# A fused attention and expert-routing kernel: V loads on ScalarE's queue, a fixed place for loads, stores and constants, and a new order of the attention stage

## The chip, the core and the metric

The kernel runs on one core of a Trainium2 chip. The engines that matter here are TensorE (PE in the profile, with its weight loads as PEld), VectorE (DVE), ScalarE (ACT), GpSimd (POOL) and SyncE (SP), which only issues DMAs in this kernel. The metric is the device time of one execution in microseconds; lower is better.

## The reference, cut to what matters

```python
def _attn_ref(q, k, v, w_phi):            # q, k, v: 8 x 8 x 576 x 64, f32
    def phi(x):
        proj = einsum('bhsd,df->bhsf', x, w_phi)               # 128 features
        proj = proj - max(abs(proj), axis=-1, keepdims=True)
        return concatenate([exp(proj), exp(-proj)], axis=-1)
    q_p, k_p = phi(q), phi(k)
    kv = einsum('bhsf,bhsd->bhfd', k_p, v)
    z = sum(k_p, axis=2)
    num = einsum('bhsf,bhfd->bhsd', q_p, kv)
    den = einsum('bhsf,bhf->bhs', q_p, z)[..., None] + 1e-06
    return num / den
```

The result, 4608 tokens of 512 numbers, goes through a mixture of eight experts: each token is assigned greedily by its largest gate logit, each expert takes at most 576 tokens, and each expert computes `relu(x @ w1) @ w2` for its own. The change touches only the attention stage; the expert stage after it has the same code before and after.

## The kernel before, in words

**Units.** The attention stage runs over 16 units, each a pair of batches and a pair of heads. The steps of a unit `u` are named in the function `unit`, and these names stand in the order table and in the prediction:

- `ldk`, `ldq`, `ldv`: the loads of k, q and v. K and Q come as eight DMAs each (L122), V as two (L128). `st` is the store of the attention output to the DRAM tensor `xs` (L313), one DMA. The input tiles `ki`, `qi`, `vi` and the output tile `xp` have two buffers each.
- `kt0`, `kt1`, `qt0`, `qt1`: 32x32 block transposes of k and q on VectorE (L175).
- `kg0` to `kg2`, `qg0` to `qg2`: the projections with w_phi on TensorE (L186), each over three of the nine token groups. Each is followed by `kgm`/`qgm`, the largest absolute value (L190, VectorE), and `kgs`/`qgs`, the subtraction (L193, VectorE). For `kg0` and `kg1`, from the second unit on, the subtraction is split: `kgc` copies out of PSUM on ScalarE (L199) and `kgs` subtracts on GpSimd (L202).
- `ke0` to `ke2`: the exponentials of k on ScalarE (L214). `ad1` to `ad8`: GpSimd's running sum of them (L222, L223). `kv0` to `kv2`: k_p times v on TensorE (L232).
- `kvt` (ScalarE, L236), `bd` (TensorE, L248), `kz` (ScalarE, L251): copy kv out, append the gate columns, copy back. `z` (TensorE, L263) folds the sum of `ad8`, and `zk` (VectorE, L265) puts it beside `kz`.
- `T0` to `T2`: transposes of the q projections on TensorE (L276), then `ex0` to `ex2`, their exponentials (ScalarE, L280).
- `num0`, `num1`: the numerator and denominator on TensorE (L293), then `x0`, `x1`, the division into `xp` on VectorE (L297, L298, L308); `lg` adds the gate logits on GpSimd (L318, L320).
- `init0` to `init18`: the routing stage's constants, a generator of small VectorE instructions and GpSimd iotas (`moe_consts`, L385 to L449), one piece at a time. `pr0` to `pr5`, `cnt0` to `cnt2` and `n0`: a part of the routing that is done early, for the first 27 of 36 token tiles.

**Order.** `Plan.order` decides the order in which instructions are emitted. Each step has an engine, a duration, dependencies and a due time; with the table `ATT['o']` present the plan is strict, so each engine takes its steps in the order of their due times, `16*u` plus the table's entry (`place`, L150). The engines run their own streams in that order and wait only on semaphores, so whatever stands behind a waiting step on its engine waits too. The table has one column for unit 0, one for unit 1, one for unit 15 and `s` for the others. PSUM for the stage is four pairs of banks, the tiles `g0` to `g3`; every TensorE step but `kv1` and `kv2` takes a pair and holds it until the step that reads it out is done.

The steady order before, from the due times in column `s` (a number after a name is the part, `+` marks a step of the next unit):

```
TensorE: kv0  kg1+ kg0+ kv1  kg2+ kv2  z  qg2+ bd  qg0+ qg1+ num0 num1 T2+ T1+ T0+
ScalarE: ke0 ke1 ke2 ex2 ex0 ex1 kgc1+ kgc0+ kvt kz
VectorE: zk  qgm0+ qgm1+ qgs0+ qgs2+ qgs1+ x0 x1 kt0++ kt1++ qt0++ qt1++ kgm1++ kgm0++ kgm2++ kgs2++ qgm2++
SyncE:   ldk 10, ldv 9, ldq 10, st 7, ldk 11, ldv 10, ldq 11, st 8, ...   (with ldq 15 between ldq 8 and st 5)
```

## Time and profile before

| | |
|---|---|
| median of 3 timed runs | 798.92 us (796.99 to 800.79) |
| the profiled execution, device time | 796.87 us |
| its span, first to last instruction | 795.1 us |
| mean granted TensorE clock | 0.978 |
| attention stage, to the end of the last `num1` | 296.1 us of the span |

The profile's page gives busy time and share by engine, the span in 40 slices of 19.9 us, and DMA queues. The timeline gives instructions in order, neighbours of one kind merged, with the idle time before them in brackets and what ended it. The chain of work follows the end of the program back, step by step, to what released it; there a stage is booked from the end of the one before it. "issue" stands where an engine waited for nothing that the profile shows.

### The profile page before, as it was taken

To read this page: it belongs to the slowest core of one execution; us is meant where nothing else is said; L and a number is where in the kernel's file an instruction comes from. 1 tells how busy PE (TensorE), PEld (TensorE's weight loads), DVE (VectorE), ACT (ScalarE), POOL (GpSimd) and SP (SyncE) were. 2 spreads that over 40 slices of the span, in tenths; PEclk is the share of its full clock that TensorE was granted. 3 is DMA by queue.
4 is the path that set the end of the run, shared out by engine and by line. 5 is a ranking of instruction groups with operands and counts; after the bars stand their busy time and mean duration, and the time that the engine had idled before them with its cause. 6 is when DMAs were issued, how large, how long until landed. Compare 5 with 4: busy or idle time off the path is not lost.

```text
span 795.1 us, 25101 instructions
## 1 busy us (share of the span) xinstructions
PE 750.4 (94%) x10718; PEld 651.2 (82%) x10718; DVE 546.5 (69%) x1343; ACT 349.4 (44%) x609; POOL 308.0 (39%) x327
## 2 busy tenths in 40 slices
PE   5999999899999986899999999999999999999995
PEld 3888888688888875598898898898898898897983
DVE  7998788598889857876686686685685685550400
ACT  2766667476766750343333333333333333441410
POOL 5887777688887850303203103104104104302011
PEclk9999999899999995899999999999999999999998
DMA  9767877867785311535505414423433334701200
GB/s 126 118 116 160 161 136 138 158 137 140 134 164 111 93 33 31 167 107 163 169 1 175 159 39 154 139 73 122 139 102 105 127 106 147 246 1 58 109 28 33
DMA packets 206655, 91.89 MB, mean 116 GB/s; under 512 B 154784, under 2 KB 189632, under 8 KB 206544
## 3 DMA queue, kind: packets, MB, share of 16 engines
q1 hardware_dynamic: 195712, 70.74, 37.5%
q0 software_dynamic: 6096, 18.97, 7.1%
q8 instruction: 84, 1.38, 0.7%
q10 hardware_dynamic: 4736, 0.59, 0.7%
q14 instruction: 27, 0.22, 0.1%
HBM read 71.39 MB, written 18.87 MB: 114 GB/s over the span
## 4 chain that ended last, share of the span: by engine, by line
PE 69%; issue 13%; DVE 5%; POOL 4%; SPq 3%; DMA 3%; ACT 1%; POOLq 0%; DVEq 0%; ACTq 0%
PE h L849 20%; PE y L878 17%; PE g L293 7%; PE g L232 7%; PE g L186 6%; SPq L122 3%; PE g L276 3%; PE y L893 2%; PE h L824 2%; POOL out_dram L907 1%; PE rps L602 1%; DMA qi<-in_q_dram 1%; POOL ks L223 1%; PE rps L598 1%; PE g L248 1%
## 5 line engine op out<-in xcount | busy, mean ns | idle before, releaser
L223 POOL TENSOR_TENSOR ks<-ks,kP 128x512 f32<-128x512 f32 x112 | 143.3, 1279 | 9.1 <-ACT kP L214 0.6
L849 PE MATMUL h<-xh,w1h 128*128 128x272 f32 (+3 forms) x512 | 144.5, 303 | 0.2 <-DVE xl L827 0.2
L849 PE MATMUL h<-xh,w1l 128*128 128x272 f32 (+3 forms) x512 | 142.9, 299 | 0.0
L907 POOL DMA_INDIRECT out_dram<-ysb,idx x40 | 40.4, 1010 | 206.2 <-ACT ysb L901 166.6
L860 ACT ACTIVATE fh<-h 128x272 fp32r<-128x272 f32 (+2 forms) x128 | 49.2, 384 | 134.7 <-PE h L849 123.6
L819 POOL DMA_INDIRECT xg<-xs,idx x40 | 39.5, 986 | 177.2 <-issue 141.3
L878 PE MATMUL y<-w2h,fl 128*128 128x512 f32 x256 | 102.1, 399 | 0.0
L878 PE MATMUL y<-w2l,fh 128*128 128x512 f32 x256 | 101.9, 398 | 0.0
L878 PE MATMUL y<-w2h,fh 128*128 128x512 f32 x256 | 101.3, 396 | 0.0
L849 PEld LDWEIGHTS h<-xh,w1h 128*128 128x128 f32 x512 | 96.4, 189 | 2.1 <-issue 1.2
L849 PEld LDWEIGHTS h<-xh,w1l 128*128 128x128 f32 x512 | 96.6, 189 | 0.0
L849 PE MATMUL h<-xl,w1h 128*128 128x272 f32 (+3 forms) x512 | 91.7, 298 | 0.0
L864 DVE SCALAR_TENSOR_TENSOR fl<-h,fh 128x272 fp32r<-128x272 f32 (+2 forms) x128 | 52.8, 420 | 55.8 <-ACT fh L860 42.4
L280 ACT ACTIVATE qP<-g 128x768 f32<-128x768 f32 x96 | 70.0, 828 | 41.9 <-PE g L276 41.9
L293 PE MATMUL g<-kz,qP 128*64 128x73 f32 x2304 | 78.5, 227 | 0.3 <-issue 0.3
L293 PEld LDWEIGHTS g<-kz,qP 128*64 128x64 f32 x2304 | 75.3, 136 | 3.7 <-issue 3.0
L214 ACT ACTIVATE kP<-kgt 128x768 f32<-128x768 f32 x96 | 72.7, 836 | 11.1 <-DVE kgt L193 10.5
L849 PEld LDWEIGHTS h<-xl,w1h 128*128 128x128 f32 x512 | 75.6, 188 | 0.0
L232 PE MATMUL g<-kP,vi 64*64 64x256 f32 x1152 | 73.2, 384 | 1.1 <-DVE xp L308 0.7
L901 ACT COPY ysb<-y 128x512 f32<-128x512 f32 (+1 forms) x40 | 21.8, 544 | 97.3 <-PE y L878 64.1
L232 PEld LDWEIGHTS g<-kP,vi 64*64 64x64 f32 x1152 | 44.1, 135 | 15.8 <-issue 3.9
L190 DVE TENSOR_REDUCE kgm<-g 128x6 f32<-128x768 f32 x48 | 44.5, 951 | 17.6 <-PE g L186 17.5
(195 smaller groups left out, 1340.1 us busy)
## 6 DMA issues: line engine op xcount, KB each, us to landing
raww<-in_moe_w_dram SPq DMA_DIRECT2D x64, 512.0 KB, 5.8
vi<-in_v_dram SPq DMA_DIRECT2D x32, 288.0 KB, 4.8
xs<-xp SPq DMA_DIRECT2D x16, 576.0 KB, 4.3
ki<-in_k_dram SPq DMA_DIRECT2D x124, 72.0 KB, 3.6
qi<-in_q_dram SPq DMA_DIRECT2D x124, 72.0 KB, 3.7
xg<-xs,idx POOLq DMA_INDIRECT x40, 3.5
out_dram<-ysb,idx POOLq DMA_INDIRECT x40, 2.9
ki<-in_k_dram ACTq DMA_DIRECT2D x4, 72.0 KB, 4.1
```

Of the source, the lines that this page charges most:

```text
L186: PE.matmul(p[64*bi:64*bi+64,a,128*(s-s0):128*(s-s0)+128],t[r,bi,s,:],C['w'][r,:],start=True,stop=True)
L190: V.tensor_reduce(m,vw(),axis=AX.X,op=OP.max,apply_absolute_value=True)
L214: for i in range(2): A.activation(o[:,:,:,128*i:128*i+128],t,AF.Exp,scale=1.0-2*i)
L223: else: G.tensor_add(ks,ks,kP[:,s])
L232: PE.matmul(p[64*a:64*a+64,i,0:256],v_[r,a,s,:],kP[r,s,a,:],start=s==0,stop=s==8,skip_group_check=True)
L280: for fh in range(2): A.activation(t[:,fh].rearrange('p a s t -> p a (s t)'),p,AF.Exp,scale=1.0-2*fh)
L293: PE.matmul(p[64*ab:64*ab+64,a,73*(j-j0):73*(j-j0)+73],T['qP',u,j//3][:,fh,a,j%3,64*ab:64*ab+64],T['kz',u][:,ab,fh,a,:],start=fh==0,stop=f ...
L849: PE.matmul(p,ws[:,k,o:o+128],xx[:,k,o1:o2],start=n==0,stop=n==11)
L860: A.activation(hh[:,f,o1:o1+m1],p[:,0:m1],AF.Relu)
L864: V.scalar_tensor_tensor(hl[:,f,o1:o1+m1],p[:,0:m1],0.0,hh[:,f,o1:o1+m1],op0=OP.max,op1=OP.subtract)
L878: PE.matmul(p,hx[:,f,o:o+128],ws[:,f%2,:],start=n==0,stop=n==23)
L907: st=G.indirect_dma_start(out=ov,out_offset=bass.IndirectOffsetOnAxis(ap=iv,axis=0),in_=yv,in_offset=None)
```

## The change

Five things change in the code. The V loads of units 1 to 15 are issued on ScalarE's queue instead of SyncE's. Every SyncE step takes its place from column `s`, in all units, so the first and the last unit's loads and stores stand where a middle unit's do. The 19 pieces of routing constants get due times of -100 to -82 and so stand first on VectorE. The planner's cost of a DMA issue, of unit 0's projections, of an init piece and of an instruction fetch (`fetch`, 3700 to 4200) change; these are numbers in the plan and no instructions. The table `o` is replaced.

```diff
@@ loadv
-            nc.sync.dma_start(t[64*i:64*i+64].rearrange('p h s d -> p h (s d)'),o)
+            (nc.scalar if u else nc.sync).dma_start(t[64*i:64*i+64].rearrange('p h s d -> p h (s d)'),o)
@@ place
-        return u*16.+t[{0:'0',1:'1',NU-1:'9'}.get(u,'s')][(name if isinstance(name,str) else ''.join(map(str,name)))+'.'+eng]
+        return u*16.+t['s' if eng=='SP' else {0:'0',1:'1',NU-1:'9'}.get(u,'s')][(name if isinstance(name,str) else ''.join(map(str,name)))+'.'+eng]
@@ unit
-            add('ldk','SP',5200.,-d['ldk'],lambda x: loadx('k',k,u),slot=slots(('ki',2)),lat=4500.)
-            add('ldq','SP',5200.,-d['ldq'],lambda x: loadx('q',q,u),slot=slots(('qi',2)),lat=4500.)
-            add('ldv','SP',1300.,-d['ldv'],lambda x: loadv(u),slot=slots(('vi',2)),lat=4500.)
+            add('ldk','SP',6000.,-d['ldk'],lambda x: loadx('k',k,u),slot=slots(('ki',2)),lat=5000.)
+            add('ldq','SP',6000.,-d['ldq'],lambda x: loadx('q',q,u),slot=slots(('qi',2)),lat=5000.)
+            add('ldv','ACT',1300.,-d['ldv'],lambda x: loadv(u),slot=slots(('vi',2)),lat=5000.)
...
-            add((nm,g),'PE',n*218.,due,pe,[(src[0]+'t',0),(src[0]+'t',1)],'Q',slots(('g',NG,nm,g)),((src,u),),ins=16*n+.5)
+            add((nm,g),'PE',n*(218. if not first else 480. if nm=='kg' else 340.),due,pe,[(src[0]+'t',0),(src[0]+'t',1)],'Q',slots(('g',NG,nm,g)),((src,u),),ins=16*n+.5)
...
-        P.add(('init',i),'DVE',330.,place(('init',i),'DVE',0,d['init']),some,[('init',i-1)] if i else [],lat=95.,after=3900.)
+        P.add(('init',i),'DVE',270.,-100.+i,some,[('init',i-1)] if i else [],lat=95.,after=3900.)
@@ ATT
...
```

The new column `s` puts the steps in this order (the same signs):

```
TensorE: kg0 kg1 kv0- kg2 qg2 kv1- qg0 kv2- qg1 bd- z- T2 T0 num0- num1- T1      (- is the unit before)
ScalarE: kgc0 kgc1 ldv ke0 kvt- kz- ke1 ex2 ex0 ke2 ex1
VectorE: kgm0 qt1 kgm1 kgm2 kgs2 qgm2 qgm0 qgs2 qgs0 kt0+ zk- qgm1 kt1+ qgs1 qt0+ x0- x1-
GpSimd:  kgs0 ad8- kgs1 ad1 ad2 ad3 ad4 lg-- ad5 ad6 ad7     (-- is two units before)
SyncE:   ldk 10, st 6, ldq 10, ldk 11, st 7, ldq 11, ...      (ldq 15 stands after st 11)
```

At the start VectorE's order is `init0` to `init12`, `kt0`, `init13`, `kt1`, `init14` to `init17`, `qt0`, `init18`, `kgm0`, `qt1` of unit 0; before, it was `init0` to `init9`, `kt0`, `kt1`, `init10`, `init11`, `kgm0`, `kgm1`, with `init12` to `init18` spread over units 1 to 4. At the end TensorE's order is `num0 num1` of unit 14, `qg1 kv0 kv1 kv2 qg2 T1 bd cnt0 cnt1 cnt2 z T2 num0 num1` of unit 15; before, `num0 num1` of unit 14, `T2 kv0 qg1 qg0 kv1 kv2 T1 T0 bd cnt0 cnt1 z cnt2 num0 num1`.

## Rows read from the trace of the kernel before

**Rows 1.** The page: busy time and share by engine with counts, the instruction queue with packets, MB and share, and one group of section 5 (busy us, mean ns of one, idle time before it).

```profile
PE 750.4 (94%) x10718; PEld 651.2 (82%) x10718; DVE 546.5 (69%) x1343; ACT 349.4 (44%) x609; POOL 308.0 (39%) x327
...
q8 instruction: 84, 1.38, 0.7%
...
L214 ACT ACTIVATE kP<-kgt 128x768 f32<-128x768 f32 x96 | 72.7, 836 | 11.1 <-DVE kgt L193 10.5
```

**Rows 2.** Busy time of each engine in a stretch of the attention stage: window, length, PE, PEld, DVE, ACT, POOL with counts, granted clock, DMA share, GB/s.

```profile
68.00:261.00 193.00, 184.11 (x4880) 162.09 (x4872) 160.42 (x248) 126.65 (x177) 150.59 (x132) 0.98 0.75 144
```

**Rows 3.** The chain of work that ended last: start, length, what. The L293 rows are `num0` and `num1` of units 2, 5, 7, 13 and 15, the L276 rows one and two of the steps `T`; the DMA row is a store of the attention output on its way.

```profile
68.41 4.72 PE g L293 x144
...
119.73 4.72 PE g L293 x144
...
141.93 3.83 DMA xs<-xp
...
159.85 4.72 PE g L293 x144
...
261.05 4.83 PE g L293 x144
...
280.69 0.80 PE g L276 x6
...
286.85 1.46 PE g L276 x12
...
291.35 4.74 PE g L293 x144
```

**Rows 4.** Timeline of TensorE's matmuls over one unit in the middle: start, length, line, operation, count. A step is read from its start to the start of the next, since the ends overlap.

```profile
172.51 0.59 PE L263 MATMUL g<-one,ks 64*64 64x2 f32 x32
172.95 0.86 PE L186 MATMUL g<-w,qT 64*64 64x128 f32 x24
173.64 0.68 PE L248 MATMUL g<-bd,kvT 64*64 64x72 f32 x32
174.14 1.83 PE L186 MATMUL g<-w,qT 64*64 64x128 f32 x48
175.90 4.79 PE L293 MATMUL g<-kz,qP 128*64 128x73 f32 x144
180.62 2.19 PE L276 MATMUL g<-ident,qgt 128*128 128x128 f32 x18
182.74 1.53 PE L232 MATMUL g<-kP,vi 64*64 64x256 f32 x24
...
187.34 1.48 PE L232 MATMUL g<-kP,vi 64*64 64x256 f32 x24
188.63 0.59 PE L263 MATMUL g<-one,ks 64*64 64x2 f32 x32
```

**Rows 5.** Timeline of ScalarE in the unit after, with the idle time before an instruction and its releaser in brackets.

```profile
186.10 1.66 ACT L199 COPY kgt<-g 128x768 f32<-128x768 f32 x2 [0.24 <-DVE kgm L190]
188.88 0.58 ACT L236 COPY kvT<-g 128x512 f32<-128x512 f32 x1 [1.12 <-PE g L232]
190.50 0.65 ACT L251 COPY kz<-g 128x576 f32<-128x576 f32 x1 [1.04 <-PE g L248]
```

**Rows 6.** Timeline of SyncE's queue from the loads of unit 8 on: start, time from the first issue of the row to the end of the last, line, count.

```profile
126.81 1.29 SPq L128 DMA_DIRECT2D vi<-in_v_dram  x2
128.21 13.68 SPq L122 DMA_DIRECT2D qi<-in_q_dram  x16
141.93 0.63 SPq L313 DMA_DIRECT2D xs<-xp  x1
```

**Rows 7.** Timeline of TensorE's matmuls in the same stretch.

```profile
146.94 1.51 PE L276 MATMUL g<-ident,qgt 128*128 128x128 f32 x6 [3.75 <-DVE rd L297]
```

**Rows 8.** Timeline of TensorE's weight loads where "issue" ended an idle time.

```profile
85.00 0.95 PEld L186 LDWEIGHTS g<-w,qT 64*64 64x64 f32 x33 [1.80 <-issue]
```

**Rows 9.** Timeline of VectorE: pieces of the routing constants.

```profile
47.40 2.07 DVE L437 TENSOR_SCALAR dup<-dup,msk 128x128 bf16<-128x128 bf16 x2
...
64.18 1.44 DVE L442 TENSOR_SCALAR idp<-idi 128x36 int32<-128x36 int32 x1 [0.86 <-POOL idi L441]
65.54 0.17 DVE L443 TENSOR_SCALAR idp<-idi 128x36 int32<-128x36 int32 x1
```

**Rows 10.** Timeline of VectorE at the start: `kt0` and `kt1` of unit 0, its `kgm0`, two of its `qgm`, the first instruction of its `x0`, and the step behind its `x1`.

```profile
9.83 1.43 DVE L175 STREAM_TRANSPOSE kT<-ki 128x576 f32<-128x576 f32 x2
...
12.92 0.96 DVE L190 TENSOR_REDUCE kgm<-g 128x6 f32<-128x768 f32 x1 [0.99 <-PE g L186]
...
21.59 1.81 DVE L190 TENSOR_REDUCE qgm<-g 128x6 f32<-128x768 f32 x2
...
36.34 0.15 DVE L297 TENSOR_SCALAR rd<-g 128x10 f32<-128x10 f32 x1
...
38.70 0.79 DVE L175 STREAM_TRANSPOSE kT<-ki 128x576 f32<-128x576 f32 x1
```

**Rows 11.** The V issues on SyncE's queue over the whole span: count, shortest, median and longest in ns, first and last start.

```profile
L128 SPq DMA_DIRECT2D vi<-in_v_dram x32: 596/632/1667, 10.7 to 257.9; - x32
```

**Rows 12.** Timeline of ScalarE's queue at the start of the program, four DMA issues to a row; SyncE's queue issues as many in the same time.

```profile
0.76 2.74 ACTq L122 DMA_DIRECT2D ki<-in_k_dram  x4
3.97 5.60 ACTq L122 DMA_DIRECT2D qi<-in_q_dram  x4
```

## The prediction

> **What bounds the kernel now.** I read the page first: TensorE is busy 94% of the span and no other engine over 69% [rows 1]. The stage that changes has the same order: from 68 to 261 us TensorE is busy 184 of 193 us, VectorE 160, GpSimd 151, ScalarE 127 [rows 2]. So what counts is the time from one unit's numerator to the next one's on TensorE. The timeline of a quiet unit gives its floor: from one `z` to the next, 172.51 to 188.63, is 16.12 us [rows 4]. The chain then says how often the floor is missed: from unit 2's numerator to unit 13's, 68.41 to 261.05, is 192.64 us [rows 3], where 11 floors are 177.3. These 15.3 us are what a new order can win in the middle; the start (VectorE nearly always busy) and the end come on top.

> Where they lie: units 5 to 7 take 40.12 us (119.73 to 159.85) [rows 3] for two floors of 32.24, so 7.9 us go at one place. There SyncE issues sixteen Q DMAs, those of unit 8 and, by its due time, of unit 15, in 13.68 us before a store; the store goes out at 141.93 [rows 6] and is 3.83 us on its way [rows 3]; VectorE's division needs its buffer, and TensorE waits 3.75 us for the division [rows 7]. The other 7.4 us, 0.68 a unit, are short idle times that end in "issue", as 1.80 us at 85.00 [rows 8], and early routing work between units 11 and 13.

> **The store's wait.** In the new order unit 15's Q loads come after unit 11's store, and V is off the queue: 17 issues a unit, at 13.68/16 = 0.86 us each [rows 6] 14.5 us, under the floor. The store of a unit follows eight K issues and its buffer is wanted two units later. The 7.9 us go; what is late next is nothing of SyncE's.

> **The split of T.** `T1` now stands behind the numerator, apart from `T2` and `T0`, one more change of form a unit. A single T took 0.80, two 1.46 [rows 3], three 2.12 (180.62 to 182.74) [rows 4]: split they cost 2.26, 0.14 more.

> **bd comes sooner after kv2.** `bd` waits for `kvt`. Before, `z` and a projection stood between; now only `qg1`, 0.66 us. `kv2` ended in issue at 188.63, `kvt` began at 188.88 and took 0.58 [rows 4, 5]; so `bd` can start about 0.88 after `kv2`, and TensorE idles 0.22. After it `z`, `T2` and `T0` hide `kz` (0.65 [rows 5]) and `zk`, which nothing hid fully before.

> **V's issues on ScalarE.** Two a unit. The trace has V only on SyncE: median 0.632, longest 1.67 [rows 11], pair 1.29 [rows 6]. ScalarE issued four in 2.74 us and four in 5.60 [rows 12], 0.69 and 1.40 each. Low 1.3, high 2.8 for the pair; I take 1.3, since the row with the same transfer is nearest. Queued behind them: `ke0`, then `kvt`, which `bd` and so TensorE waits for. From the start of `kg0` as zero: `kg0` and `kg1` end at 1.3; VectorE's two maxima with `qt1` between end at 3.5; the second `kgc` (0.83, [rows 5]) ends at 4.4; V's issues end at 5.7; `ke0`, two of 0.84 [rows 1], ends at 7.3. TensorE's `kv2` ends at 7.2 (seven projections or so of 0.66 and three kv of 1.29 [rows 4]), so `kvt` is due at 7.4. The issues are hidden with 0.1 to spare, and every further 0.1 us is a 0.1 us later `bd` in every unit.

> **Short "issue" idle times.** 84 packets of 16.4 KB went to the instruction queue, and TensorE ran 2 x 10718 instructions [rows 1]: 255 to a packet, an estimate. If TensorE must wait for the next block when it runs through one fast, dense stretches cost. Before, `z`, `qg2`, `bd`, `qg0` (224 instructions) pass from 172.51 to about 175.0 [rows 4], so 255 take 2.9 us. Now the densest stretch is part of `qg0`, then `kv2`, `qg1`, `bd`, `z`: 0.4 + 1.29 + 0.66 + 0.50 + 0.44 = 3.3, with the wait for `kvt` 3.5. The cost lies between 0 and the 0.68 a unit above; I take 0.23.

> **A unit after:** 16.12 + 0.14 + 0.22 + 0.23 = 16.71. Eleven are 183.8; with 0.5 for the early routing work, which stands between `kt1` and `zk` and still delays a numerator, 184.3 against 192.64: **-8.3**.

> **The start.** All constants now stand on VectorE ahead of unit 0's `kgm0`. Beside GpSimd's sums two of them took 2.07 us and one 1.44 after a wait of 0.86, while one of the same shape took 0.17 [rows 9]; up front GpSimd has little to do, and I cost what moves at some 15 instructions near 0.17. `kgm0` moves from 12.92 [rows 10] to about 15.2. From there to `x0` of unit 0 VectorE has 21 reductions and subtractions at 0.87 and five transposes at 0.72 (half of 21.59's and 9.83's pairs, less their overlap [rows 10]): 22.0, so `x0` at 37.2 instead of 36.34, with one step more done. To `qgs0` of unit 2 come nine at 0.87, four transposes and two divisions (2.36 from 36.34 to 38.70 [rows 10]): 13.1, so 50.3; `T0` and unit 1's numerator at 51.3; unit 2's at about 67.9 against 68.41 [rows 3]: **-0.5**. Bounds: the 2.3 us of delay carried whole (70.7), or all of the slow constants' time won (64).

> **The end.** From unit 13's numerator to the end of unit 15's is 35.04 us (261.05 to 296.09 [rows 3]). TensorE's work there is the same but for `T2` and `T0` of unit 14, which now stand ahead of unit 13's numerator: two of 0.66 less: **-1.2**, if `ad8`, GpSimd's last sum, isn't late for `z`.

> **Sum:** -8.3 - 0.5 - 1.2 = -10.0, against the profiled execution's own 796.87: 786.9. The median of the timed runs, 798.92, lies 2.05 above that execution; half of this is added: **788**.

> **The rivals.**

> *ScalarE's queue is held (slower).* If an issue there waits while SyncE's queue issues, the pair takes up to 4 x 0.632 = 2.5 us, and at the start's slow pace, 2 x 1.40 = 2.8 [rows 11, 12]. Then `ke0` ends at 8.6 to 8.9, `bd` starts at 9.2 to 9.5 instead of 8.05, and 13 units lose 1.15 to 1.45 each: 15 to 19 us, 802 to 806. It decides from 2.2 us a pair, where 13 x 0.77 takes the 10 us back. For it: the 5.60 row. Against it: the 2.74 row, issued while SyncE issued as many. [...] Chance 0.17, of which 0.12 ends slower by over 0.5%.

> *The "issue" idle stays as it was.* 0.68 a unit instead of 0.23: 5 us, 793. For it: the densest stretch, 3.3 us, is only 0.4 longer than before. Chance 0.12.

> *The start's delay is carried.* Unit 2 at 70.7: 791. For it: VectorE has no idle time there to absorb 2.3 us. Chance 0.08.

> *The change doesn't take the stall away.* Another late load or store in the fixed order costs the same 7.9 once: 796. Against it: 14.5 us of issues in 16.7. Chance 0.07.

> *No new waits at all:* 16.3 a unit: 783 or less. Chance 0.06.

> **How the numbers follow.** The forecast, with its own range of 785 to 791, has the remaining 0.50. About 0.5%, 4 us, is what a measurement here can tell from no change, so 795 to 803 is the same. Faster: 0.50 + 0.12 + 0.08 + 0.06 = 0.76. Same: the stall's 0.07 and 0.05 of the held queue, 0.12. Slower: 0.12. The range reaches from 781, without the new waits and with the start's better bound in part, to 798, the stall kept and a little more; outside lie the held queue's 0.17 and little else.

> **What would show it.** Right: numerators 16.4 to 17.0 us apart from unit 2 to unit 13 with no gap of several us near unit 7; V pairs of 1.3 us on ScalarE; a TensorE gap of 0.2 to 0.3 before `bd` put down to `kvt`; `kgm0` of unit 0 at about 15; unit 13's numerator near 252. Wrong: V issues over 1 us each with `bd` waiting over a microsecond; numerators 17.5 apart; "issue" gaps of over a microsecond in `qg1` or `bd`; a division that waits for `xs` again.

## The result, and the profile after

The changed kernel takes 803.55 us (median of 9 runs, 801.2 to 804.65) against 798.86 for the kernel before in the same sessions: a ratio of 1.0057, 95% interval 1.0033 to 1.0081. It is slower by 4.7 us where 788 was forecast. Its profiled execution is 802.43 us with a span of 800.5; the span before was 795.1. Of the four runs with V on GpSimd (median 792.14 below) one, of 1153.36 us, fell into a slower state, and its ratio leaves that run out; the median of the other three is 791.81.

The page of the changed kernel; the rows of before are in [rows 1].

```profile
PE 750.5 (94%) x10718; PEld 651.6 (81%) x10718; DVE 543.5 (68%) x1343; ACT 352.3 (44%) x609; POOL 306.1 (38%) x327
...
PEclk7969999999999996799999999999999999999998
...
L293 PE MATMUL g<-kz,qP 128*64 128x73 f32 x2304 | 80.3, 230 | 12.4 <-ACT kgt L199 11.2
```

Busy times hardly moved. What is new stands in the last column of the last row: the numerators (L293) waited 12.4 us in all, 11.2 of them for one instruction of ScalarE, the copy `kgc` of L199. PEclk shows the place, a 6 in the third slice of 20 us. Stretches of 5 us there (window, length, PE, PEld, DVE, ACT, POOL, granted clock, DMA share, GB/s):

```profile
35.00:40.00 5.00, 1.18 (x38) 1.03 (x34) 4.93 (x9) 0.00 (x0) 0.00 (x0) 0.85 0.55 85
40.00:45.00 5.00, 0.00 (x0) 0.00 (x0) 0.30 (x1) 0.00 (x0) 0.00 (x0) 0.50 0.72 113
```

From 40 to 45 us no engine computes but VectorE, for 0.30 us, and the granted clock falls to 0.50; from 172 to 188 us, in a quiet unit, it is 1.00. It stays at 0.50 until 52 us: the 64 matmuls of the numerator's second part take 4.16 us, where all 144 of a later one take 4.79. The timeline of TensorE's matmuls there, and its numerators of units 2 and 13:

```profile
33.42 2.76 PE L293 MATMUL g<-kz,qP 128*64 128x73 f32 x80
47.35 4.16 PE L293 MATMUL g<-kz,qP 128*64 128x73 f32 x64 [11.17 <-ACT kgt L199]
51.44 1.87 PE L276 MATMUL g<-ident,qgt 128*128 128x128 f32 x12
...
81.80 2.38 PE L293 MATMUL g<-kz,qP 128*64 128x73 f32 x68
...
266.41 4.79 PE L293 MATMUL g<-kz,qP 128*64 128x73 f32 x144
```

The numerator of unit 0 is cut in two. Unit 2's starts at 81.80 and was at 68.34 before (its row in the chain [rows 3] starts 0.07 later, here as there). From it to unit 13's are 184.61 us; before they were 192.64. So the difference of the two spans has this sum: +13.5 at the start, -8.0 in the middle, -0.4 from unit 13 to the end of unit 15's numerator (34.73 against 35.08), +0.3 behind it: +5.4. The middle gave the number that was forecast; the start lost more than that.

Who holds ScalarE is read from its timeline and from SyncE's, in that order:

```profile
31.04 1.58 ACT L214 ACTIVATE kP<-kgt 128x768 f32<-128x768 f32 x2 [0.47 <-POOL kgt L202]
44.30 2.10 ACTq L128 DMA_DIRECT2D vi<-in_v_dram  x2
46.50 0.80 ACT L199 COPY kgt<-g 128x768 f32<-128x768 f32 x1 [13.88 <-DMA qi<-in_q_dram]
```

```profile
30.29 7.37 SPq L122 DMA_DIRECT2D qi<-in_q_dram  x8
37.76 5.29 SPq L122 DMA_DIRECT2D ki<-in_k_dram  x8
43.15 6.36 SPq L122 DMA_DIRECT2D qi<-in_q_dram  x8
```

ScalarE is done with `ke` at 32.62 and issues nothing until V of unit 1 at 44.30 and 45.78; the copy stands behind these two and waits 13.88 us, put down to the landing of a **Q**. The chain says the same from the other end:

```profile
43.15 2.60 DMA qi<-in_q_dram
45.76 0.02 issue
45.78 0.62 ACTq L128
...
46.50 0.81 ACT kgt L199
...
47.35 4.16 PE g L293 x64
```

An issue of V that waits for a Q has no buffer in common with it. The reason stands in the trace's semaphores: each DMA issue carries the number of the one that tells of its landing. Four of these issues, in us (not a view of the profile):

```
SP   L122 ki<-in_k_dram   semaphore 107   out 41.75, landed 44.28   (7th of K, unit 3)
ACT  L128 vi<-in_v_dram   semaphore 107   out 44.30                 (V, unit 1)
SP   L122 qi<-in_q_dram   semaphore 111   out 43.15, landed 45.76   (1st of Q, unit 3)
ACT  L128 vi<-in_v_dram   semaphore 111   out 45.78                 (V, unit 1)
```

In this trace the DMAs of SyncE and of ScalarE carry eight semaphores between them, 107, 109, 111 and 113 to 117, in turn, 46 DMAs to each. None of the 360 issues that have a predecessor on their semaphore starts before that one has landed. Ahead of the seventh and the eighth Q of unit 3 SyncE's sequence leaves out 107 and 111, which V's two have. So V's two have their turns just before and just after the seventh Q of unit 3. On its semaphore V's first issue comes behind the seventh K of unit 3 (K3), which went out at 41.75 and landed at 44.28; the second behind the first Q of unit 3 (Q3), out at 43.15, landed at 45.76. V went out 0.02 us after each. In the order of before, V of unit 1 stood ahead of K of unit 2 and went out at 23.65; the new order fetches K and Q two units ahead and gives V its turn behind K of unit 3. SyncE's queue issues from 10.88 to 55.97 with no pause over 0.12 us and can't be there sooner.

The hold costs more than its 11.17 us. From unit 0's numerator to unit 1's are 31.79 us (33.42 to 65.21); in the same order with V on GpSimd, an experiment below, they are 18.53. The difference is 13.3. The 2.1 us beyond the wait are nearly all in the numerator's second part: 64 matmuls in 4.09 us (47.35 to 51.44) at a granted clock of 0.50, where 64 of 144 in 4.79 would be 2.1.

The rows of the issues don't show the hold: the 30 issues of V on ScalarE show 602 to 1376 ns, median 620, and none shows the 11 us that the queue stood.

### The profile page after: what moved, and what is told of

The parts are those of the page before. It is cut to its first block, busy times and chain, and to the rows that moved or that the text cites. A ratio compares the mean times of both kernels' runs of the same rounds, so it can differ in the third digit from the quotient of the medians.

```text
span 800.5 us, 25106 instructions
## 1 busy us (share of the span) xinstructions
PE 750.5 (94%) x10718; PEld 651.6 (81%) x10718; DVE 543.5 (68%) x1343; ACT 352.3 (44%) x609; POOL 306.1 (38%) x327
## 4 chain that ended last, share of the span: by engine, by line
PE 71%; issue 13%; DVE 5%; SPq 4%; DMA 3%; POOL 2%; ACT 1%; POOLq 0%; ACTq 0%; DVEq 0%
PE h L849 20%; PE y L878 17%; PE g L293 8%; PE g L232 7%; PE g L186 6%; PE g L276 4%; SPq L122 3%; PE y L893 2%; DMA qi<-in_q_dram 2%; PE h L824 2%; POOL out_dram L907 1%; PE rps L602 1%; PE g L248 1%; PE rps L598 1%; DMA raww<-in_moe_w_dram 1%
## 5 line engine op out<-in xcount | busy, mean ns | idle before, releaser
L293 PE MATMUL g<-kz,qP 128*64 128x73 f32 x2304 | 80.3, 230 | 12.4 <-ACT kgt L199 11.2
L293 PEld LDWEIGHTS g<-kz,qP 128*64 128x64 f32 x2304 | 76.9, 138 | 16.3 <-ACT kgt L199 11.3
L214 ACT ACTIVATE kP<-kgt 128x768 f32<-128x768 f32 x96 | 75.5, 840 | 21.9 <-DVE kgt L193 10.1
L280 ACT ACTIVATE qP<-g 128x768 f32<-128x768 f32 x96 | 72.4, 809 | 24.6 <-PE g L276 14.1
L232 PE MATMUL g<-kP,vi 64*64 64x256 f32 x1152 | 70.4, 377 | 0.4 <-DMA ki<-in_k_dram 0.4
L878 PEld LDWEIGHTS y<-w2h,fh 128*128 128x128 f32 x256 | 48.2, 188 | 9.1
L878 PEld LDWEIGHTS y<-w2l,fh 128*128 128x128 f32 x256 | 48.3, 189 | 8.7
```

The source lines that it names most:

```text
L214: for i in range(2): A.activation(o[:,:,:,128*i:128*i+128],t,AF.Exp,scale=1.0-2*i)
L232: PE.matmul(p[64*a:64*a+64,i,0:256],v_[r,a,s,:],kP[r,s,a,:],start=s==0,stop=s==8,skip_group_check=True)
L280: for fh in range(2): A.activation(t[:,fh].rearrange('p a s t -> p a (s t)'),p,AF.Exp,scale=1.0-2*fh)
L293: PE.matmul(p[64*ab:64*ab+64,a,73*(j-j0):73*(j-j0)+73],T['qP',u,j//3][:,fh,a,j%3,64*ab:64*ab+64],T['kz',u][:,ab,fh,a,:],start=fh==0,stop=f ...
L878: PE.matmul(p,hx[:,f,o:o+128],ws[:,f%2,:],start=n==0,stop=n==23)
```

## The experiments

Theory T: V's turn behind a late DMA of SyncE's holds ScalarE, and that alone lost the start. Its rivals: ScalarE pays for each issue whatever the order (Q), or the new order is too tight at its start whichever queue has V (O). In the expectations, theory L is T's first form.

**V of unit 1 earlier on ScalarE.** Two places for it, first in the queue and in between.

```
-'1': {'ldv.ACT': -6.785, ...
+'1': {'ldv.ACT': -230.0, ...     # first run;  -70.0 in the second
```

> The changed kernel, with one number altered: unit 1's V load stands first on ScalarE, ahead of unit 0's exponentials. Theory L (completion semaphores in turn): the DMAs of SyncE's and ScalarE's queues share eight completion semaphores in the order in which the program was written, and each waits until the DMA eight places before it has landed; in the changed kernel unit 1's two V issues stand behind the seventh K and the first Q DMA of unit 3. Here they stand behind unit 0's Q loads instead, so they go out at 10 to 12 us; ScalarE isn't held after ke0 of unit 1, num1 of unit 0 follows num0 at once, unit 1's numerator starts at 51 to 54, unit 13's near 253, time 787 to 791. Theory Q (ScalarE's issue is held because SyncE's queue is busy issuing): the V issues are held at the start too, ke0 of unit 0 starts several us late, and the time stays at 798 or more.

> The changed kernel, with unit 1's V load moved only a little earlier on ScalarE, to behind the first exponential of q of unit 0 (about 25 us). In the turn of the completion semaphores it then stands behind the first and second K DMA of unit 3, which SyncE issues at 37.8 and 38.4. Theory L: though it stands earlier, it is held longer: ScalarE stands from about 25 to 42, with kvt of unit 0 behind it, so bd of unit 0 and everything after it waits; unit 0's numerator starts near 50 instead of 33.4 and the time is 806 to 822. Theory Q: an earlier place can't be worse; ScalarE is held at most as long as in the changed kernel, time 795 to 803.

First in the queue: 806.28 us, ratio 1.0088 [1.0056, 1.0120]. V went out at 10.78 and 11.48, as expected, and the numerator of unit 0 ran through, 34.66 to 39.45. The time didn't follow, because V of unit 2 took over the part. ScalarE's timeline, then TensorE's:

```profile
57.41 1.47 ACTq L128 DMA_DIRECT2D vi<-in_v_dram  x2
58.93 0.58 ACT L236 COPY kvT<-g 128x512 f32<-128x512 f32 x1 [12.10 <-DMA ki<-in_k_dram]
```

```profile
59.57 1.24 PE L248 MATMUL g<-bd,kvT 64*64 64x72 f32 x32 [10.09 <-ACT kvT L236]
```

Unit 2's numerator started at 82.17, as late as with the change. In between (a single run, 805.82 us), V was held, as expected behind the first two DMAs of K3, until 38.61 (the copy `kvt` behind it waited 14.77 us, put down to a K), and TensorE waited 13.88 us for `kvt`. An earlier place gave a longer hold. So T says rightly what V waits for, and was wrong that V of unit 1 is all there is; Q, which had the time of the first run in its range, needed V held at the start, and it wasn't.

**V of unit 2 off ScalarE too.**

```
+V of unit 1 at -230.0 as above
-(nc.scalar if u else nc.sync).dma_start(...)
+(nc.scalar if u not in (0,2) else nc.sync).dma_start(...)
```

> Changed kernel, with V of unit 1 first on ScalarE's queue and V of unit 2 alone put on SyncE's queue at its place there; V of units 3 to 15 stay on ScalarE. Theory L (the whole loss is two held issues on ScalarE, V of unit 1 and then V of unit 2): V of unit 1 goes out near 10.8, the numerator of unit 0 runs from 34.7 to 39.5, V of unit 2 goes out on SyncE at about 51 and lands near 56, TensorE waits for nothing over 2 us between 30 and 70, the numerator of unit 1 starts at 52 to 56 and that of unit 2 at 68 to 72; from there as in the changed kernel with V of unit 1 first (219.3 us from unit 2's numerator to the end of the attention), time 788 to 796. Rival O (the searched order is too tight at the start whichever queue holds V, and the wait moves on to the next transfer): a wait of 5 us or more in units 1 to 4 again, time 800 or more.

804.09 us, ratio 1.0066 [1.0038, 1.0093]. Unit 1's numerator started at 53.78, as expected; then V of unit 3 was held. ScalarE's timeline, SyncE's, TensorE's:

```profile
73.66 2.18 ACTq L128 DMA_DIRECT2D vi<-in_v_dram  x2
75.88 1.57 ACT L214 ACTIVATE kP<-kgt 128x768 f32<-128x768 f32 x2 [12.18 <-DMA ki<-in_k_dram]
```

```profile
68.79 5.30 SPq L122 DMA_DIRECT2D ki<-in_k_dram  x8
```

```profile
77.98 1.24 PE L248 MATMUL g<-bd,kvT 64*64 64x72 f32 x32 [10.63 <-ACT kvT L236]
```

Three times the same: TensorE waits 10 to 11 us once, at the first V that isn't freed, and unit 2's numerator is at 82 to 83. After the hold, ScalarE comes later than SyncE and no V waits long. So it is not one place in the order: ScalarE is set back once to where SyncE's queue has got to. This looks like rival O, and the next two runs part O from T.

**V on another queue, in the new order.**

```
-(nc.scalar if u else nc.sync).dma_start(...)
+nc.sync.dma_start(...)                        # first run
+(nc.gpsimd if u else nc.sync).dma_start(...)  # second run
```

> The changed kernel with all V loads on SyncE's queue, the rest of its order kept. Theory L: unit 1's V issues now follow unit 2's Q loads on SyncE at about 37.8 and land near 43; ScalarE is free, num1 of unit 0 follows num0 at once, TensorE waits 2 to 6 us for V at kv0 of unit 1; unit 1's numerator at 54 to 58. In the middle SyncE has 19 issues a unit, 16.3 us at 0.86, just under the unit: 16.6 to 17.0 a unit. Time 791 to 797. Rival (the constants up front or the new start order is what holds unit 1): the start is as late as in the changed kernel, time 800 to 804.

> Changed kernel, with V of units 1 to 15 issued from GpSimd's queue, at the place in the order that ScalarE had for it. Theory T (V is held because its completion semaphore is one of the eight that SyncE's and ScalarE's DMAs use in turn, and SyncE's queue is behind at the start; DMAs of GpSimd use other semaphores): no V is held anywhere, V of unit 1 goes out when GpSimd comes to it (33 to 37), the wait doesn't pass on to V of units 2 and 3 as it did with V freed on ScalarE, numerators of units 0, 1 and 2 start at about 33.5, 52 to 55 and 68 to 71.5, units 2 to 13 stay at 183 to 187 us, time 786 to 793. Rival O (the new order is too tight at its start and some transfer is always late): a wait of 5 us or more of TensorE in units 0 to 4, time 799 or more. Rival G (GpSimd, 150.6 of 192.7 us busy in the middle, becomes late by the issues of V): no single wait, but units 2 to 13 over 190 us, time 795 or more.

On SyncE: 801.42 us, ratio 1.0023 [1.0005, 1.0041]. Unit 1's numerator started at 55.45 and unit 2's at 71.97, so ScalarE's hold is gone, and with it the late start that the rival needed, though the time is in the rival's range and not in L's 791 to 797. But V of unit 5 stands behind eight Q on a queue without a gap, and `kv` waits for it; SyncE, then TensorE:

```profile
109.07 6.92 SPq L122 DMA_DIRECT2D qi<-in_q_dram  x8
116.10 1.31 SPq L128 DMA_DIRECT2D vi<-in_v_dram  x2
```

```profile
120.29 3.66 PE L232 MATMUL g<-kP,vi 64*64 64x256 f32 x22 [7.57 <-DMA vi<-in_v_dram]
```

On GpSimd, whose DMAs carry other semaphores in the trace (99 to 106): **792.14 us, ratio 0.9919 [0.9898, 0.9940]**, faster than the kernel before and than the changed one. V goes out when GpSimd comes to it, and the wait isn't passed on; GpSimd's timeline:

```profile
30.95 1.23 POOL L128 DMA_DIRECT2D vi<-in_v_dram  x2
...
46.16 1.19 POOL L128 DMA_DIRECT2D vi<-in_v_dram  x2
```

Numerators of units 0, 1 and 2 start at 33.43, 51.96 and 69.34; the prediction had 51.3 and 67.9 for the last two. T stands, and O falls in its strong form. But units 2 to 13 take 189.45, not 183 to 187: the last period is 24.21. SyncE's timeline, then VectorE's, ahead of unit 13's numerator:

```profile
215.33 8.92 SPq L122 DMA_DIRECT2D ki<-in_k_dram  x8
224.35 0.58 SPq L313 DMA_DIRECT2D xs<-xp  x1
225.03 6.78 SPq L122 DMA_DIRECT2D qi<-in_q_dram  x8
231.91 7.95 SPq L122 DMA_DIRECT2D ki<-in_k_dram  x8
```

```profile
239.92 0.78 DVE L175 STREAM_TRANSPOSE kT<-ki 128x576 f32<-128x576 f32 x1 [3.13 <-DMA ki<-in_k_dram]
...
247.18 0.78 DVE L175 STREAM_TRANSPOSE qT<-qi 128x576 f32<-128x576 f32 x1 [4.08 <-DMA qi<-in_q_dram]
```

17 issues, 215.33 to 231.91, take 16.58 us, more than a quiet unit of TensorE's, 16.16. SyncE had 0.4 us of pauses (over 0.1 us each) between 70 and 255 (6.3 in the changed kernel), fell behind by a few tenths a unit, and at last K and Q of unit 14 were late. Without the hold, SyncE's queue is the pace.

Not all of the gain is the attention's. Its last numerator ends at 294.49, against 301.14 after the change and 296.06 before: 6.65 and 1.6 us. Another 4.9 us lie behind the last output DMA. In spans of 789.0 and 800.5 us it starts at 785.28 here and at 791.84 in the changed kernel:

```profile
785.28 0.97 POOL L907 DMA_INDIRECT out_dram<-ysb,idx  x1 [2.34 <-ACT ysb L901]
```

```profile
791.84 0.97 POOL L907 DMA_INDIRECT out_dram<-ysb,idx  x1 [2.34 <-ACT ysb L901]
```

GpSimd's closing drain, a DRAIN instruction at the end of its stream, takes 3.16 us here, and 8.06 in every kernel whose V isn't on GpSimd.

**The queue alone, in the order of before.**

```
-nc.sync.dma_start(...)                        # loadv of the kernel before
+(nc.scalar if u else nc.sync).dma_start(...)  # first run
+(nc.gpsimd if u else nc.sync).dma_start(...)  # second run
```

> Kernel before with its own order, and V of units 1 to 15 issued from ScalarE's queue at the place in the order that it has now: that part of the change alone. Theory T: V of unit 1 has its turn ahead of K of unit 2 here (in the changed order it comes behind K of unit 3), so the transfer it waits for landed by 23 to 25; it goes out at 22.5 to 25 and holds ScalarE no more than 2.5 us; V of unit 2 may be held up to 4 us; the numerator of unit 1 starts no later than 53, the stall at units 5 to 7 stays, time 793 to 802. Rival Q (issuing V from ScalarE costs by itself, whatever the order: ScalarE held 5 us or more in the first units or in each unit): numerator of unit 1 after 57 or units over 17.5 apart outside the stall, time 804 or more.

> Kernel before with its own order, V of units 1 to 15 issued from GpSimd's queue: with the run of V on ScalarE in the old order (822.7) and V on GpSimd in the new order (792.1) this tells what the queue costs and what the order is worth. Theory T (ScalarE's holds alone made 822.7; the new order, without the held start, is worth 5 to 8 us): V is held nowhere, the stall at units 5 to 7 stays at 5 to 8 us, the numerator of unit 1 at 50 to 54, time 795 to 802, like before. Rival (the old order is as good as the new one when V leaves both queues): 789 to 793. Rival G (issues of V disturb GpSimd in the old order): units over 17.5 apart outside the stall, time over 804.

On ScalarE: 822.67 us, ratio 1.0315 [1.0286, 1.0344], 20 us over what T was taken to say. Here V is held in nearly every unit: in units 1 to 7 its second DMA goes out 2.3 to 5.5 us after ScalarE's last instruction, in units 8 to 13 1.0 to 3.4. Units 2 to 5 are 22.1 to 22.4 apart. ScalarE, then SyncE:

```profile
116.92 1.26 ACTq L128 DMA_DIRECT2D vi<-in_v_dram  x2
118.22 0.64 ACT L251 COPY kz<-g 128x576 f32<-128x576 f32 x1 [5.02 <-DMA qi<-in_q_dram]
```

```profile
113.35 5.87 SPq L122 DMA_DIRECT2D qi<-in_q_dram  x8
```

In this order V's turn comes behind the first two Q of the same burst, out at 113.35 and 113.97, and ScalarE is there while they are under way, so it waits out their landing; in units 1 to 7 V stands behind two Q each time. That was T's mechanism with a dose that I had put at 2.5 to 4 us in two units. Q's numbers came out, but not Q's reason: the same 30 issues show 602 to 889 ns here, median 614.

On GpSimd in the old order: 798.97 us, ratio 0.9987 [0.9960, 1.0013], as T expected. Its closing drain is 3.16 us too, so the attention took longer (its end at 301.01). Between the two orders with V on GpSimd lie 6.8 us by the medians (798.97 - 792.14), 5.4 by the two ratios, each against its own session's kernel before, and 6.5 us in the attention's end (301.01 - 294.49): so the new order is worth some 5 to 7 us once V isn't held.

**The early Q15.** The load alone moved, then its reader with it.

```
-'ldq.SP': -106.932,          # both runs, table of the last unit, kernel before
+'ldq.SP': 1.917,
-'qt0.DVE': -14.733,          # second run only
+'qt0.DVE': 16.4,
```

> The kernel before, with one number altered: unit 15's Q loads stand where a middle unit's do, ahead of unit 14's store turn and no longer between unit 8's loads and unit 5's store. The step of the prediction: the wait of the division for the store and the slow clock behind it, 7.9 us between units 5 and 7, go and nothing takes their place: numerators of units 5 and 7 32 to 33.5 us apart, time 789 to 792. Rival (SyncE's queue is late anyway): another store or load is late by as much, time 795 to 799.

> Kernel before, with the load of unit 15's Q at the place in the order that Q has in the middle units, and this time its reader, the transpose of that Q on VectorE, moved along with it (right behind the key maxima of unit 15). Theory S (the early Q15 alone made the stall at units 5 to 7, 6.3 to 8 us, and nothing but its reader made the new stall at unit 12): numerators of units 5 to 7 33.5 apart instead of 40.1, no wait over 3 us at unit 12, time 790 to 793. Rival N (the order of before has no room for a later Q15 at its end): a stall of 5 us or more at units 12 to 15 stays, time 798 or more.

The load alone: 809.56 us, ratio 1.0141 [1.0108, 1.0173]. Units 5 to 7 fell from 40.12 [rows 3] to 33.58, as expected, and a new wait came at unit 12:

```profile
250.08 7.44 PE L293 MATMUL g<-kz,qP 128*64 128x73 f32 x144 [13.33 <-DVE kz L265]
```

VectorE's order still had the transpose of Q15 where the early load had let it be, between the work of units 13 and 14, and waited there for the late load. With the reader moved: 795.5 us, ratio 0.9955 [0.9930, 0.9981]; units 5 to 7 are 34.90 apart, no wait over 1 us is left at unit 12. The time lies between the two theories' ranges: some 4 us are won (0.45%, by the interval 0.2 to 0.7), not 7.9. Units 2 to 13 took 189.04, against 192.64 before, but that is one profile each, and the next run, which keeps the early Q15, had 189.31 there; where the rest went isn't shown.

**The constants alone**, in the kernel before.

```
-P.add(('init',i),'DVE',330.,place(('init',i),'DVE',0,d['init']),...)
+P.add(('init',i),'DVE',330.,-200.+i,...)
```

> Kernel before, with the routing constants alone put at the head of VectorE's order; loads, stores and attention as before. Theory C (the constants are cheap at the head, where VectorE has nothing to do, and cost some 3 us of VectorE's time at their places of before): first key maxima of unit 0 at 12.9 to 15.5, numerator of unit 2 no later than 68.3 and up to 1.5 earlier, time 797 to 799. Rival: the constants at the head push the start back by their own 2.5 to 3 us, and the numerator of unit 1 starts at 52.5 or later, time 800 to 802.

A single run: 798.24 us; `kgm0` at 15.68, numerators of units 1 and 2 at 54.18 and 70.30. The time is the theory's, the starts are the rival's; but the two kernels above that keep the old start (Q15 with reader, V on GpSimd) had unit 2 at 70.98 and 70.93 in their profiles, so 2 us of scatter between executions covers the difference. Inconclusive. They also say that the 68.34 of before was an early one, and that the change's true loss at the start is nearer 11 than 13.5.

**SyncE relieved further.**

```
-eng.dma_start(...)           # raw(), with V on GpSimd as above
+(nc.gpsimd if u and x is q and a and db else eng).dma_start(...)       # first run
+(nc.gpsimd if 8<=u<14 and x is q and a and db else eng).dma_start(...) # second run
```

> As with V on GpSimd's queue, and two of the eight DMAs of each unit's Q (the last quarter of either half) issued from GpSimd as well. With V on GpSimd the start is mended (unit 2 at 69.3 instead of 81.8), but SyncE has no idle time left between 70 and 255 (0.4 us; 187 issues of 0.895 us mean), and the period u12 to u13 is 24.2 with VectorE waiting for K of unit 14. Theory P (SyncE's own number of issues is what it is short of): 15 instead of 17 issues per unit give SyncE 1.3 to 1.8 us of idle time per unit, no period over 18 from unit 2 to 13, units 2 to 13 at 182 to 186, time 783 to 789. Rival R (the issues are slowed by what all queues share, and the mean issue grows when their number falls, as it did from 0.796 to 0.91 us when V left SyncE): mean issue on SyncE 1.0 us or more, a late K or Q somewhere still, time 790 to 795. Rival G (the waits for a free Q buffer hold GpSimd): key work on GpSimd late, gaps of 2 us or more at kgt, time over 795.

> As with V on GpSimd's queue, and two of the eight DMAs of Q issued from GpSimd for units 8 to 13 alone (with all units it cost GpSimd 18 us more busy time between 68 and 261, 183.6 of 193, and brought nothing: 793.3). Theory P (with V on GpSimd the only loss left in the middle is SyncE's queue falling behind until K of unit 14 is late): SyncE gains some 9 us until then, the period u12 to u13 falls from 24.2 to 16.2 to 18, no other grows by more than 1, time 783 to 789. Rival G (each issue that GpSimd takes comes back as late key work, whichever units it is in): periods of units 8 to 13 at 17 or more, time 790 to 794.

793.26 us, ratio 0.9934 [0.9904, 0.9964], and 793.75, ratio 0.9932 [0.9914, 0.9951]: no gain over 792.14 (the intervals overlap), and neither reaches P's 783 to 789. Busy times from 68 to 261 us with V alone on GpSimd, then with two Q more:

```profile
68.00:261.00 193.00, 185.49 (x4943) 163.95 (x4944) 159.86 (x250) 132.53 (x181) 165.32 (x156) 0.98 0.79 143
```

```profile
68.00:261.00 193.00, 185.38 (x5064) 164.14 (x5058) 162.97 (x246) 135.04 (x184) 183.57 (x180) 1.00 0.78 144
```

In the first run SyncE had 35.5 us of pauses and the period before unit 13 was 16.15, so P was right on SyncE (mean issue 0.831 us, so not R, which had the right time); GpSimd went from 165 to 184 busy us of 193, and units 2 to 8 grew to 16.4 to 18.6. The 8.1 us that the period before unit 13 gave were nearly all spent: 5.1 between units 2 and 12, where ScalarE now waits 9.4 us for GpSimd's subtractions from 70 to 175 us, a wait that V alone didn't bring, and 2.7 between units 13 and 14, where TensorE waits 3.05 us for VectorE's subtraction of q. That GpSimd's lateness made all of the 5.1 isn't shown: TensorE's own idle rows there end in "issue" or in `kvt`. SyncE's issues between 70 and 255 fell from 167.4 to 133.8 us, and the time didn't fall. In the second run the period before unit 13 fell from 24.2 to 16.97 and the attention ended at 291.54, the earliest of all, but other periods grew (units 8 to 13 are 16.2 to 17.8 apart, where G had 17 or more), a wait of 2.10 us for the same subtraction stands behind unit 13, and the closing drain took 6.43 us. Why that drain varies wasn't tried.

## Why the prediction was wrong

**The step that failed: V's issues on ScalarE.** It took an issue to cost what its row shows, 1.3 us a pair, and asked whether that is hidden in a middle unit, which it is. It never asked which DMA the issue has to wait for. The cost was a wait of 11.17 us, once, and 13.3 with the slow clock behind it, in a unit that the working of the start passes by looking at VectorE alone: its list from `kgm0` to unit 1's numerator has no instruction of ScalarE's. The rest of that list held: `kgm0` at 14.69 (15.2), `x0` of unit 0 at 36.74 (37.2), and with V on GpSimd units 1 and 2 at 51.96 and 69.34 (51.3, 67.9). The constants that were slow in between are as cheap up front as thought; VectorE's timeline after the change:

```profile
13.06 0.42 DVE L437 TENSOR_SCALAR dup<-dup,msk 128x128 bf16<-128x128 bf16 x2
```

0.42 for the two that took 2.07 [rows 9].

**The rival that was near.** "ScalarE's queue is held" gave 802 to 806 and 803.55 came, but by another mechanism. It had a longer issue in each unit, which no run shows: V's median is 620 ns beside SyncE's issues (614 in the old order), and the longest pair that isn't held, from 243.01 us on, takes 2.0 us, under the 2.2 from which this rival decides. What was held was ScalarE itself, for 11.7 us (32.62 to 44.30), until a DMA of SyncE's had landed. The row that I put for this rival, four Q in 5.60 us [rows 12], was the sign that I misread. In the changed kernel's trace ScalarE's four Q go out at 3.92, 7.08, 7.81 and 9.16; the four K before them on the same semaphores landed at 3.90, 7.06, 7.79 and 9.14. Even the trace of before has such pairs, 5.63 behind a landing at 5.61 and 7.61 behind 7.59. They waited their turn.

**The middle, -8.3: -8.0 came, with its parts off.** The wait for the store is gone; the five idle times that TensorE's timeline shows from 82 to 266 us, 0.25 to 1.60 us long, all end in "issue". Of the 7.9 us that the prediction booked on that wait, 3.75 were the wait itself [rows 7]; behind it, from 146 to 152 us of the trace of before, the granted clock was 0.50, and the prediction has no word on that. A smaller stall stands at the same place now. The two periods from unit 5 to 7 are 16.69 and 19.85, and the second is 3.7 over a quiet unit:

```profile
164.73 0.75 PE L263 MATMUL g<-one,ks 64*64 64x2 f32 x19 [1.60 <-issue]
165.41 2.82 PE L276 MATMUL g<-ident,qgt 128*128 128x128 f32 x12
168.17 4.80 PE L293 MATMUL g<-kz,qP 128*64 128x73 f32 x144
```

After a gap of 1.60 the granted clock is 0.50 from 165 to 168, and `T2` and `T0` take 2.76 instead of 1.46. The quiet unit behind it:

```profile
180.92 0.83 PE L186 MATMUL g<-w,qT 64*64 64x128 f32 x24
181.81 0.73 PE L248 MATMUL g<-bd,kvT 64*64 64x72 f32 x32
182.36 0.59 PE L263 MATMUL g<-one,ks 64*64 64x2 f32 x32
182.88 1.53 PE L276 MATMUL g<-ident,qgt 128*128 128x128 f32 x12
184.34 1.36 PE L293 MATMUL g<-kz,qP 128*64 128x73 f32 x36
```

`bd` starts 0.89 after `qg1`, 0.24 more than a projection takes (0.22 forecast). T split costs 0.81 + 1.46 = 2.27 (2.26). Yet the unit is 16.17 long, not 16.12 + 0.36. The missing 0.3 is probably the cover of `kz` and `zk`, named in the working and given no number: before, 48 projections in front of the numerator took 1.76 [rows 4], 0.45 more than their 1.31. What lies above eleven quiet units is 184.61 - 177.87 = 6.7. Of this 3.7 are the one period; the other ten have 3.1, or 0.31 a unit, where 0.23 + 0.05 was forecast. So a quiet unit 0.3 shorter than forecast and a stall that the forecast hadn't cancel out: that -8.0 came is luck. It is also one profile against one: the kernel before with only the constants moved takes 189.31 from unit 2 to 13, 4.7 more than the changed kernel and not 8.0.

**"What is late next is nothing of SyncE's": wrong, and hidden.** I took 0.86 us an issue, 14.5 a unit. Without V the mean issue of SyncE's went from 0.796 to 0.910 us between 70 and 255, and 17 with their gaps of 0.04 fill 16.15. The changed kernel doesn't show it; the likely reason is that the hold at the start, which set the units back by 12.5 us (81.80 against 69.34 with V on GpSimd), gave SyncE's queue that lead. Where the start was mended it cost 5 us in the middle (189.45 against the forecast 184.3).

**The end, -1.2: -0.35.** Two of 0.66 are 1.32, not 1.2, which doesn't matter here. Two idle times of TensorE's behind unit 13's numerator, 0.50 and 0.49 us, are put to VectorE, whose order has 4.6 us of routing work (265.12 to 269.71) ahead of `qgm` and the division.

So the hold was not the only miss. With V on GpSimd nothing is held, and the attention still ends only 1.6 us earlier than before, where 10.0 were forecast: +1.0 to unit 2's numerator (69.34 against 68.34), -3.2 to unit 13's, +0.6 to the end. The first two rest on that early 68.34: four other kernels with the attention's old order and V held nowhere have 69.80 to 70.98, against which the start is 0.5 to 1.6 earlier, the way that was forecast; how a gain divides between start and middle can't be told from one profile each. The 792.14 us owe more to the closing drain than to the attention.

## What to carry to other kernels

A DMA that is moved to the queue of a computing engine can bring a wait that the row of its issue doesn't show; here ScalarE stood for 11.7 us ahead of an issue of 0.67. Look up which earlier DMA has its completion semaphore, where that one stands on its own queue, and when it lands; what stood behind the moved issue waited as well. Read such a wait from the gap before the next instruction (13.88 us), not from the issue's duration. Count a long wait of TensorE with the slow clock behind it, which made 13.3 us of 11.17 here. Before counting on a freed wait, look for the queue that has no idle time left, here SyncE's with 0.4 us of pauses between 70 and 255: it took the gain back, one transfer further on each time. And a load that is moved to a later place needs its reader moved too: Q15 without it brought a wait of 13.33 us.
